# A planner that counts TensorE's instructions as they arrive, and a third MLP block begun in another bank

## The chip, the cores and the metric

The kernel runs on one core of one Trainium2 chip. The metric is device time in microseconds (us) of one execution. Engines are called as in the profile: PE is TensorE (PEld its weight loads), ACT is ScalarE, DVE is VectorE, POOL is GpSimd, SP is SyncE, whose queue issues nearly all DMAs here.

## The reference

```python
def _attn_ref(q, k, v):                       # (8 batch entries, 8 heads, 576, 64)
    scores = 1.0 / np.sqrt(D) * np.matmul(q, k.transpose(0, 1, 3, 2))
    rel = pos[:, None] - pos[None, :]
    mask_plain = (rel >= 0) & (rel < 32)                       # heads 0 to 3
    mask_dil = (rel >= 0) & (rel < 128) & (rel % 4 == 0)       # heads 4 to 7
    scores = np.where(masks[None], scores, -1e9)
    attn = softmax(scores)                    # maximum taken off, sum + 1e-9 below
    return np.matmul(attn, v)
def _moe_ref(x, w_in, w_out):                 # x (4608, 512), w_in (512, 2048), w_out (2048, 512)
    h = x @ w_in
    g = h * (1.0 / (1.0 + np.exp(-1.702 * h)))
    return g @ w_out
```

The MLP reads the attention's output, tokens by 512 (8 heads of 64). q, k and v are f32, the weights f64.

## The kernel before

**The MLP** is the bulk of the work. Each f32 operand is split into a high and a low part that PE can multiply at full rate (`xh`, `xl` of the tokens, `wih`, `wil`, `woh`, `wol` of the weights, `gh`, `gl` of the gated values), and each product is made of three matmuls (high·high, low·high, high·low). Tokens go in groups of 512: `m0` to `m7` are the first 512 tokens of the eight batch entries, `r` is the 64 left of each, 8 x 64. The inner dimension of 2048 goes in 16 blocks `f`. `Group.up(f)` makes 12 matmuls (four chunks `c` of 128 inputs, three each) into the PSUM tile `hp`; ACT takes the tanh of it (L613), DVE the gate (L616), ACT or DVE the high part `gh` (L234 or L236), DVE or POOL the low part `gl` (L241). `Group.down(f)` adds 12 matmuls into four accumulators `acc`. There is one `hp` bank, so `up(f + 1)` waits for the gate of `f`; in the first group alone, `f == 1` uses the bank `sp`, which is otherwise the attention's scores.

**The weights** arrive as f64 words cut into u64, and each of the 32 tiles (`decode(n)`, even `n` w_in, odd `n` w_out) is decoded on the way in: three ACT passes (L289, L290, L283; the last can be a DVE one, L285), then on DVE a shift (L293) and an add (L295), a cast to the high part (ACT or DVE) and a subtraction for the low part (L241, DVE or POOL). Five buffers hold raw tiles: `cell0` to `cell2`, and the two halves of `second`; two more raw tiles pass through `bt` and the buffer `qk`. All decoding falls into the first group's time.

**The attention** of one batch entry is four pairs of heads (`k`, four for each entry). `scores` (L369 for the mask, L383, 88 or 76 small matmuls) write `sp`; DVE takes maximum (L402), subtracts (L241), ACT the exponential (L406), DVE the sum (L420), its reciprocal (L410, L412), POOL or DVE multiplies `pr` by it, DVE transposes into `ct`. For the first entry, `first_product` (L470) multiplies `ct` by `v` straight into `first_x`, four PSUM banks that hold the outputs of two pairs in turn; ACT copies the high part `xh` out of it, DVE subtracts for `xl`. The first entry's four pairs must be through before the first group's four chunks are there. Later entries go through `bt` and the bank `av` (L484), and run beside the group before them.

**The order.** `Plan` holds every step with a cost for each engine that may run it, an urgency, what it reads and writes. `ordered` plays the engines forward with these costs and lists the steps in the order in which they would start; each engine's program is then fixed in that order, and an engine that waits for one step's input holds back all steps behind it. SP's DMAs are steps of the same list. `LATER` adds to the planned end of a step on an engine when an engine is chosen for it, and `AHEAD` lets an urgent step be waited for. Where PE is planned to have nothing for over half a microsecond, and the planned time is below `WARM`, `ordered` puts in idle products (`warm`, L727: `ident` times `ident` into the unused bank `av`, 512 columns), which keep PE's clock up.

## Time and profile before

| | |
|---|---|
| runs before, median of 3 (lowest to highest) | 900.85 us (900.6 to 901.49) |
| the profiled execution's own time | 900.52 us |
| its span, first to last instruction | 898.4 us |
| mean granted clock of PE | 0.992 |
| PE busy, share of the span | 98% |
| DVE, ACT, POOL busy | 51%, 43%, 6% |

A row of the timeline gives start, duration and the number of like instructions that follow one another; in brackets stands how long the engine had been idle and who ended that. "issue" means that it waited for nothing that the profile shows. Matmul durations overlap (a row of 0.39 us starts 0.23 us after the one before it), so PE's pace is read from the starts. In the table of stretches PEclk is the granted clock of PE, 1.00 being full speed.

### The profile page before, as it was taken

Reading aid. Unit: us, or ns where it says so; the run is one execution under the profiler, and the core shown is the slowest. Engines: PE = TensorE matmul, PEld = TensorE weight load, DVE = VectorE, ACT = ScalarE, POOL = GpSimd, SP = SyncE. Lnnn points to the kernel's source line nnn. Section 1 sums busy time; section 2 is a strip of 40 time slices with the busy share of each in tenths; the row PEclk is TensorE's granted clock in tenths of the full one; section 3 lists DMA queues with packets and bytes.
Section 4 is the critical chain, followed back from the end, with each engine's and each line's share of the span. In section 5 each row is a group of like instructions: output and inputs, shape, how many; then the busy total and the mean of one; then the engine's idle time right before and its main releaser. Section 6 shows DMA issues by size and latency. Waiting matters only on the chain.

```text
span 898.4 us, 17202 instructions
## 1 busy us (share of the span) xinstructions
PE 883.9 (98%) x7352; PEld 718.3 (80%) x7352; DVE 461.6 (51%) x858; ACT 390.1 (43%) x680; POOL 50.2 (6%) x61
## 2 busy tenths in 40 slices
PE   7899999999999999999999999999999999999998
PEld 4577878888888888888888888888888888888886
DVE  5899986666566336652566255634622322232222
ACT  6888984343443234432543245333532322232222
POOL 2131001000001001000000000000100000000000
PEclk9899999999999999999999999999999999999999
DMA  9358743131223003110331022200100010002001
GB/s 356 101 179 254 196 171 125 48 93 47 71 71 94 1 9 133 48 47 0 96 92 47 1 94 60 81 1 20 49 1 1 1 47 1 1 1 47 1 1 47
DMA packets 35804, 61.34 MB, mean 68 GB/s; under 512 B 17424, under 2 KB 17680, under 8 KB 35728
## 3 DMA queue, kind: packets, MB, share of 16 engines
q1 hardware_dynamic: 35584, 60.11, 21.0%
q8 instruction: 58, 0.95, 0.5%
q14 instruction: 18, 0.15, 0.1%
q10 hardware_dynamic: 144, 0.13, 0.0%
HBM read 49.48 MB, written 9.44 MB: 66 GB/s over the span
## 4 chain that ended last, share of the span: by engine, by line
PE 92%; ACT 3%; DMA 2%; DVE 2%; issue 1%; SPq 0%; DVEq 0%; ACTq 0%
PE hp_m L605 38%; PE acc_m L641 13%; PE acc_m L642 13%; PE acc_m L645 12%; PE hp_r L605 5%; PE av L484 3%; PE sp L383 3%; PE acc_r L642 2%; PE acc_r L641 2%; PE acc_r L645 2%; DMA cell<-wi_dram 1%; DMA second<-wi_dram 1%; ACT words L289 0%; PE first_x L470 0%; PE sp L484 0%
## 5 line engine op out<-in xcount | busy, mean ns | idle before, releaser
L605 PE MATMUL hp_m<-xh,wih 128*128 128x512 f32 x512 | 201.5, 394 | 2.9 <-ACT woh L234 2.2
L641 PE MATMUL acc_m<-gh,woh 128*128 128x512 f32 x512 | 201.6, 394 | 0.3 <-ACT gh L234 0.3
L616 DVE SCALAR_TENSOR_TENSOR g_m<-g_m,hp_m 128x512 f32<-128x512 f32 x128 | 87.7, 685 | 220.7 <-ACT g_m L613 220.5
L605 PE MATMUL hp_m<-xh,wil 128*128 128x512 f32 x512 | 200.1, 391 | 0.0
L605 PE MATMUL hp_m<-xl,wih 128*128 128x512 f32 x512 | 199.9, 391 | 0.0
L642 PE MATMUL acc_m<-gh,wol 128*128 128x512 f32 x512 | 199.8, 390 | 0.0
L613 ACT ACTIVATE g_m<-hp_m 128x512 f32<-128x512 f32 x128 | 76.5, 597 | 247.0 <-PE hp_m L605 242.8
L645 PE MATMUL acc_m<-gl,woh 128*128 128x512 f32 x512 | 143.4, 391 | 0.0
L605 PEld LDWEIGHTS hp_m<-xh,wih 128*128 128x128 f32 x512 | 96.2, 188 | 24.6 <-ACT woh L234 2.6
L241 DVE TENSOR_TENSOR gl<-g_m,gh 128x512 fp32r<-128x512 f32 x126 | 89.8, 713 | 50.7 <-ACT gh L234 49.4
L641 PEld LDWEIGHTS acc_m<-gh,woh 128*128 128x128 f32 x512 | 96.5, 189 | 21.4 <-ACT gh L234 0.7
L605 PEld LDWEIGHTS hp_m<-xl,wih 128*128 128x128 f32 x512 | 96.4, 188 | 20.4 <-DVE xl L241 0.3
L605 PEld LDWEIGHTS hp_m<-xh,wil 128*128 128x128 f32 x512 | 96.4, 188 | 20.2 <-DVE wil L241 0.7
L642 PEld LDWEIGHTS acc_m<-gh,wol 128*128 128x128 f32 x512 | 96.6, 189 | 19.7
L645 PEld LDWEIGHTS acc_m<-gl,woh 128*128 128x128 f32 x512 | 95.5, 188 | 20.1
L234 ACT ACTIVATE gh<-g_m 128x512 fp32r<-128x512 f32 x113 | 71.2, 630 | 67.5 <-DVE g_m L616 67.4
L241 POOL TENSOR_TENSOR pr<-pr,sm 128x320 f32<-128x320 f32 x45 | 40.1, 901 | 546.6 <-DVE sm L412 541.8
L234 ACT ACTIVATE bt<-ct 32x320 f32<-32x320 f32 x102 | 47.9, 470 | 11.1 <-DVE ct L433 9.3
L406 ACT ACTIVATE pr<-pr 128x640 f32<-128x640 f32 x32 | 23.7, 740 | 41.1 <-DVE pr L241 40.5
L616 DVE SCALAR_TENSOR_TENSOR g_r<-g_r,hp_r 128x512 f32<-128x512 f32 x16 | 11.0, 687 | 50.7 <-ACT g_r L613 50.7
L234 ACT ACTIVATE xm<-av 128x512 f32<-128x512 f32 (+2 forms) x42 | 23.7, 596 | 28.8 <-PE av L484 16.6
L420 DVE TENSOR_REDUCE sm<-pr 128x10 f32<-128x640 f32 x32 | 26.1, 816 | 16.7 <-ACT pr L406 16.7
(119 smaller groups left out, 839.0 us busy)
## 6 DMA issues: line engine op xcount, KB each, us to landing
qk<-qk_dram SPq DMA_DIRECT2D x17, 576.0 KB, 4.5
out_dram<-ost_m SPq DMA_DIRECT2D x31, 256.0 KB, 2.1
second<-qk_dram SPq DMA_DIRECT2D x13, 576.0 KB, 5.0
v<-vp_dram SPq DMA_DIRECT2D x32, 216.0 KB, 4.6
words<-vp_dram SPq DMA_DIRECT2D x24, 216.0 KB, 4.3
cell<-wi_dram SPq DMA_DIRECT2D x10, 512.0 KB, 6.6
cell<-wo_dram SPq DMA_DIRECT2D x9, 512.0 KB, 5.6
second<-wo_dram SPq DMA_DIRECT2D x6, 512.0 KB, 4.9
```

What stands on the lines that cost most here:

```text
L234: A.activation(dst, src, AF.Copy, scale=scale)
L241: (V if e == DVE else G).tensor_tensor(out=dst, in0=a, in1=b, op=op)
L383: T.matmul(dst[:, w:w + n], u["qk"][rows, at:at + 32], u["qk"][rows, S + first:S + first + n], start=not masked(k), stop=True, tile_positi ...
L406: add({ACT: 0.75}, urgency, lambda e: A.activation(prs[y], prs[y], AF.Exp, scale=0.125), (), (PR,))
L420: add({DVE: 0.80}, urgency, lambda e: V.tensor_reduce(out=sm, in_=pr, axis=AX.X, op=ALU.add), (PR,), (SM,))
L484: T.matmul(dst, u["v"][a][0:KW, m], bt[0:KW, a, m], start=True, stop=True, skip_group_check=True)
L605: T.matmul(hps[f], st[:, f, c], mv[:, c], start=c == 0 and k == 0, stop=c == NC - 1 and k == 2)
L613: A.activation(self.g32, hps[f], AF.Tanh, scale=0.851)
L616: V.scalar_tensor_tensor(out=self.g32, in0=self.g32, scalar=1.0, in1=hps[f], op0=ALU.add, op1=ALU.mult)
L641: T.matmul(self.acc[j], woh[:, f, cols], gh, start=f == 0, stop=False)
L642: T.matmul(self.acc[j], wol[:, f, cols], gh, start=False, stop=False)
L645: T.matmul(self.acc[j], woh[:, f, P * j:P * j + P], self.g[f][1], start=False, stop=f == NF - 1)
```

## The change

Four things are edited. (1) The planner gets a model of PE's instructions arriving in blocks: steps of PE carry a `count` of instructions, and `fetched` lets a step that crosses an edge (193, then every 256) begin its rest no sooner than the next block is there. (2) Idle products that are planned before 12 us are of 128 columns and four times as many. (3) In the first group, block `f == 2` goes into the bank `av`, and the second entry's attention and the last eight decodes, which stood behind block 1, stand behind block 2; idle products end where this block starts. (4) The planner's numbers change: `AHEAD`, `WARM`, DVE's entry of `LATER`, and the urgencies of the first loads, of the decodes (`32.0 + 1.92 * n` for `28.0 + 2.62 * n`) and of the second entry's attention (`52.0 + 9.4 * c` for `43.0 + 8.2 * c`).

```diff
-AHEAD = 0.70
-WARM = 36.0
+AHEAD = 0.36
+WARM = 60.0
+SHORT = 12.0
...
-LATER = {PE: 0.0, ACT: 0.0, DVE: 0.40, POOL: 0.0, DMA: 0.0}
+LATER = {PE: 0.0, ACT: 0.0, DVE: 0.49, POOL: 0.0, DMA: 0.0}
...
+        issued, blocks = [0], [0.0]
...
+        def fetched(count, when, cost):
+            n = issued[0]
+            issued[0] += count
+            for j in range(len(blocks) - 1, 1 << 30):
+                edge = 193 + 256 * j
+                if edge >= n + count or edge > 1500:
+                    return when + cost
+                part = cost * (edge - n) / count
+                at = max(when + part, blocks[j])
+                blocks.append(at + (6.1 if at < 18.0 else 4.2))
+                when, cost, n, count = at, cost - part, edge, count - (edge - n)
...
-                idle = max(0, int((when - max(free[e], 1.2) - 0.5) / (0.26 if when > 8.0 else 0.44)))
-                order.extend([(None, e)] * idle)
+                short = when < SHORT
+                size = (0.26 if when > 8.0 else 0.44) * (0.25 if short else 1.0)
+                idle = max(0, int((when - max(free[e], 1.2) - 0.5) / size))
+                fetched(2 * idle, max(free[e], 1.2), idle * size)
+                order.extend([(None if short else -1, e)] * idle)
             order.append((i, e))
+            if e == PE:
+                cost = fetched(ops[i][5], when, cost) - when
...
-        add({DMA: 524}, {0: -8.1, 1: -6.2, 2: -5.2, 3: -4.5}.get(n, urgency), fetch, (), (R, R + "l", *taken))
+        add({DMA: 524}, {0: -8.6, 1: -7.4, 2: -5.1, 3: -2.2}.get(n, urgency), fetch, (), (R, R + "l", *taken))
...
-        add({DMA: 590}, (-9.0, -8.0, -6.0, -4.0)[k] if k < NC else 1.6 * k - 2.0, work, waits(k), (place, place + "l"))
+        add({DMA: 590}, (-9.0, -6.6, -3.2, -2.1)[k] if k < NC else 1.6 * k - 2.0, work, waits(k), (place, place + "l"))
...
-        add({DMA: 390 if k < NC else 442}, (-5.5, -3.0, -2.0, -1.0)[k] if k < NC else 1.6 * k - 0.3, work, waits(k),
-            (place, place + "l"), (0.0, 1.0, 5.0, 14.0)[k] if k < NC else 0.0)
+        add({DMA: 390 if k < NC else 442}, (-7.8, -6.4, -4.9, -1.4)[k] if k < NC else 1.6 * k - 0.3, work, waits(k),
+            (place, place + "l"), (0.0, 0.0, 4.0, 6.0)[k] if k < NC else 0.0)
...
-            place = "sp" if self is main[0] and f == 1 else "hp"
+            place = {1: "sp", 2: "av"}.get(f, "hp") if self is main[0] else "hp"
...
-                decode(n, 28.0 + 2.62 * n)
+                decode(n, 32.0 + 1.92 * n)
...
-            if nxt == 1 and f == 1:
+            if nxt == 1 and f == 2:
                 for c in range(NC):
-                    attention(NC + c, 43.0 + 8.2 * c)
+                    attention(NC + c, 52.0 + 9.4 * c)
...
-    def warm(e):
-        if "av" not in pairs[NC]:
+    def warm(i):
+        if 2 not in main[0].hps:
             if "idle" not in misc:
                 misc["idle"] = bank([P, GT], "av", "idle")
-            T.matmul(misc["idle"], ident, ident[:, None, :].broadcast_to([P, GT // P, P]), start=True, stop=True)
+            n = 1 if i is None else GT // P
+            T.matmul(misc["idle"][:, 0:P * n], ident, ident[:, None, :].broadcast_to([P, n, P]), start=True, stop=True)
```

Smaller edits: the first entry's steps get counts of 180 and 184 and new costs (1.5, and 2.3 for the first, in place of 1.6 and 2.1), the MLP's steps counts of 6, 4 and 2; the first two decodes' urgencies are 1.0 higher. Lines of the changed kernel are 22 to 24 further down than those of the profile.

The edits work through the order. PE's program has 98 more instructions of idle products ahead of the third pair's scores: 20, 43 and 8 products (two instructions each) before the scores of pairs 0, 1 and 2, where there were 5, 7 and 10; the idle products that stood before the first pair's product (6) are gone.

SP's first loads before (`qk_0`, `second`, `xm`, `xr` are the queries and keys of pairs 0 to 3; `v_0` and the second load of `second` are the values of pairs 0 and 1; `cell0`, `cell2` and `cell1`, `bt` are raw w_in and w_out tiles 0 and 1):

```order
L326 DMA qk_0_124<-qk_dram 128x1152
L279 DMA cell0_112<-wi_dram 128x512
L326 DMA second_111<-qk_dram 128x1152
L279 DMA cell1_113<-wo_dram 128x512
L326 DMA xm_76<-qk_dram 128x1152
L339 DMA v_0_130<-first_v_dram 128x768
L279 DMA cell2_114<-wi_dram 128x512
L279 DMA bt_86<-wo_dram 128x512
L326 DMA xr_77<-qk_dram 128x1152
```

and now:

```order
L348 DMA qk_0_124<-qk_dram 128x1152
L301 DMA cell0_112<-wi_dram 128x512
L361 DMA v_0_127<-first_v_dram 128x768
L301 DMA cell1_113<-wo_dram 128x512
L348 DMA second_111<-qk_dram 128x1152
L361 DMA second_111<-first_v_dram 128x768
L301 DMA cell2_114<-wi_dram 128x512
L348 DMA xm_76<-qk_dram 128x1152
L301 DMA bt_86<-wo_dram 128x512
L348 DMA xr_77<-qk_dram 128x1152
```

The queries and keys of pair 1 moved from third to fifth place, behind the values of pair 0 and the raw w_out tile 0; those of pair 2 from fifth to eighth; w_in tile 1 (`cell2`) stays seventh.

DVE before, from the reciprocal of pair 1's sums (`sm1`) to that of pair 2's (`sm0`); `xr` and `xl` read pair 0's product, the transposes make pair 1's `ct`:

```order
L412 RECIPROCAL sm1_83<-sm1_83 128x10
L241 TENSOR_TENSOR pr1_79<-pr1_79,sm1_83 128x320
L236 COPY xr_77<-first_x_90 128x64
L429 STREAM_TRANSPOSE ct1_85<-pr1_79 128x320
L241 TENSOR_TENSOR xl_71<-first_x_90,xh_70 128x432
L241 TENSOR_TENSOR xl_71<-first_x_90,xh_70 128x80
L429 STREAM_TRANSPOSE ct1_85<-pr1_79 128x320
L420 TENSOR_REDUCE sm0_82<-pr0_78 128x10
L402 TENSOR_REDUCE mx1_81<-sp_3_397 128x10
L410 TENSOR_SCALAR sm0_82<-sm0_82 128x10
L241 TENSOR_TENSOR pr1_79<-sp_3_397,mx1_81 128x640
L412 RECIPROCAL sm0_82<-sm0_82 128x10
```

and now, over the same stretch:

```order
L434 RECIPROCAL sm1_83<-sm1_83 128x10
L317 ISA words_115<-cell2_114,words_115 128x1024
L315 TENSOR_SCALAR words_115<-words_115 128x512
L442 TENSOR_REDUCE sm0_82<-pr0_78 128x10
L263 TENSOR_TENSOR xl_71<-first_x_90,xh_70 128x432
L263 TENSOR_TENSOR xl_71<-first_x_90,xh_70 128x80
L451 STREAM_TRANSPOSE ct1_85<-pr1_79 128x320 x2
L424 TENSOR_REDUCE mx1_81<-sp_3_442 128x10
L432 TENSOR_SCALAR sm0_82<-sm0_82 128x10
L263 TENSOR_TENSOR pr1_79<-sp_3_442,mx1_81 128x640
L434 RECIPROCAL sm0_82<-sm0_82 128x10
```

The sum of pair 2 (`sm0<-pr0`) stood behind four steps that read pair 0's product or its high part; now it stands ahead of them, and POOL does both of pair 1's multiplications, and ACT the copy to `xr`.

PE before, from the first block's last chunk (`hp_m0_0`; `hp_m0_1` and `hp_m0_2` are the second and third block):

```order
L605 MATMUL hp_m0_0_454<-xh_70,wih_66 128x512
L605 MATMUL hp_m0_0_454<-xh_70,wil_67 128x512
L605 MATMUL hp_m0_0_454<-xl_71,wih_66 128x512
L605 MATMUL hp_m0_1_655<-xh_70,wih_66 128x512
L605 MATMUL hp_m0_1_655<-xh_70,wil_67 128x512
L605 MATMUL hp_m0_1_655<-xl_71,wih_66 128x512
L605 MATMUL hp_m0_2_698<-xh_70,wih_66 128x512
L605 MATMUL hp_m0_2_698<-xh_70,wil_67 128x512
L605 MATMUL hp_m0_2_698<-xl_71,wih_66 128x512
L641 MATMUL acc_m0_0_708<-gh0_72,woh_68 128x512
L642 MATMUL acc_m0_0_708<-gh0_72,wol_69 128x512
```

and now:

```order
L628 MATMUL hp_m0_0_506<-xh_70,wih_66 128x512
L628 MATMUL hp_m0_0_506<-xh_70,wil_67 128x512
L628 MATMUL hp_m0_0_506<-xl_71,wih_66 128x512
L628 MATMUL hp_m0_1_569<-xh_70,wih_66 128x512
L628 MATMUL hp_m0_1_569<-xh_70,wil_67 128x512
L628 MATMUL hp_m0_1_569<-xl_71,wih_66 128x512
L628 MATMUL hp_m0_2_714<-xh_70,wih_66 128x512
L628 MATMUL hp_m0_2_714<-xh_70,wil_67 128x512
L628 MATMUL hp_m0_2_714<-xl_71,wih_66 128x512
L628 MATMUL hp_m0_3_756<-xh_70,wih_66 128x512
L628 MATMUL hp_m0_3_756<-xh_70,wil_67 128x512
L628 MATMUL hp_m0_3_756<-xl_71,wih_66 128x512
```

Before, one chunk of the third block stood behind the last chunks of the first two, in the bank of the first, and the accumulation of block 0 followed; now three chunks of the third block are already done at this place, its fourth follows, and two chunks of a fourth block come before the accumulation.

More of the change, by code (lines that the diff above doesn't have):

```diff
@@ L47, in __init__, with add @@
         self.ops, self.writer, self.readers = [], {}, {}
-    def add(self, costs, urgency, work, reads=(), writes=(), slack=0.0):
+    def add(self, costs, urgency, work, reads=(), writes=(), slack=0.0, count=0):
         i, after = len(self.ops), set()
@@ L133, in ordered @@
                         open_[to].add(j)
-        return [(warm if i is None else ops[i][2], e) for i, e in order]
+        return [(ops[i][2] if i is not None and i >= 0 else lambda e, i=i: warm(i), e) for i, e in order]
 @with_exitstack
```

17 lines of the change are left out of this document (9 added, 8 removed).

## The prediction

> **What bounds the kernel now.** I read the page's shares first, then PE's waits, then a table of stretches (its columns: stretch, length, busy time of PE, PEld, DVE, ACT, POOL, granted clock, DMA share, GB/s), then the timelines where PE lost time.
>
> ```profile
> span 898.4 us, 17202 instructions
> ...
> PE 883.9 (98%) x7352; PEld 718.3 (80%) x7352; DVE 461.6 (51%) x858; ACT 390.1 (43%) x680; POOL 50.2 (6%) x61
> ```
>
> ```profile
> PE hp_m L605 <- ACT woh L234: 2.2, 1, 2.2
> PE first_x L470 <- issue: 1.9, 1, 1.9
> ...
> PE sp L383 <- issue: 1.1, 1, 1.1
> ```
>
> ```profile
> 10.00:20.00 10.00, 7.24 (x247) 4.37 (x247) 8.20 (x17) 7.37 (x10) 3.97 (x4) 0.99 1.02 407
> 20.00:30.00 10.00, 8.73 (x231) 5.61 (x231) 6.01 (x15) 6.29 (x12) 1.40 (x2) 0.50 0.35 124
> ...
> 40.00:50.00 10.00, 7.84 (x27) 5.59 (x25) 9.01 (x18) 8.20 (x13) 0.00 (x0) 0.83 0.60 175
> ...
> 117.00:135.00 18.00, 16.98 (x72) 12.96 (x71) 17.38 (x33) 15.98 (x29) 0.00 (x0) 1.00 0.37 121
> 135.00:800.00 665.00, 665.00 (x5302) 549.15 (x5301) 320.43 (x596) 251.01 (x465) 27.97 (x31) 1.00 0.15 46
> ```
>
> PE bounds it: from 135 to 800 us it is never idle, at full clock. The change takes no work out of that stretch, so the time moves only by what PE loses before 135. Three losses can be read there: the first entry's attention, in which PE waits twice for nothing that the profile shows ("issue") and runs at half clock from 20 to 30; a wait of 2.2 before the third MLP block, with the clock at 0.83 about it; and 1.0 of idle time from 117 to 135, while DVE is busy 17.38 of 18 us and ACT 15.98. The 98% hides the first of these, because idle products count as busy.
>
> ```profile
> 6.66 3.15 PE L727 MATMUL idle<-ident 128*128 128x512 bf16 x7
> 9.62 0.46 PE L369 MATMUL sp<-plain,ident 128*128 128x320 bf16 x2
> ...
> 14.06 1.10 PE L383 MATMUL sp<-xm 64*32 64x32 f32 x88
> ...
> 17.46 0.77 PE L470 MATMUL first_x<-ct,v 32*64 32x32 f32 x50 [0.67 <-DVE ct L429]
> 20.18 0.92 PE L470 MATMUL first_x<-ct,v 32*64 32x64 f32 x40 [1.95 <-issue]
> ...
> 24.18 0.24 PE L383 MATMUL sp<-xr 64*32 64x16 f32 x2 [1.09 <-issue]
> ...
> 25.92 1.67 PE L470 MATMUL first_x<-ct,second 32*64 32x32 f32 x92
> ...
> 31.77 1.08 PE L470 MATMUL first_x<-ct,xm 32*64 32x64 f32 x80
> ...
> 35.89 1.08 PE L470 MATMUL first_x<-ct,xr 32*64 32x64 f32 x80 [0.77 <-DVE xl L241]
> ...
> 41.06 0.40 PE L605 MATMUL hp_m<-xl,wih 128*128 128x512 f32 x1
> 43.62 0.62 PE L605 MATMUL hp_m<-xh,wih 128*128 128x512 f32 x1 [2.16 <-ACT woh L234]
> ...
> 47.25 0.40 PE L642 MATMUL acc_m<-gh,wol 128*128 128x512 f32 x1
> ...
> 112.69 1.15 PE L484 MATMUL av<-bt,v 96*64 96x64 f32 x32
> ...
> 122.01 0.39 PE L605 MATMUL hp_m<-xh,wih 128*128 128x512 f32 x1
> ...
> 123.83 0.39 PE L605 MATMUL hp_m<-xl,wih 128*128 128x512 f32 x1
> ```
>
> The last two rows are eight matmuls apart: 0.2275 us each at full speed. The two "issue" rows cut steps in the middle. With two instructions a product, 700 stand ahead of the first cut in PE's order (28 idle products, 270 of three scores, 52 of pair 0's product) and 956 ahead of the second: 256 apart. So I take it that code comes in blocks, with edges at 444 and 1212 too. Instruction 444 ran near 14.2, 20 products into pair 2's scores; the block behind 700 came at 20.18, 6.0 later, while loads ran at 407 GB/s, and the next 4.0 after that.
>
> ```profile
> 40.80 0.60 ACT L613 ACTIVATE g_m<-hp_m 128x512 f32<-128x512 f32 x1
> ```
>
> ```profile
> 42.80 0.68 DVE L616 SCALAR_TENSOR_TENSOR g_m<-g_m,hp_m 128x512 f32<-128x512 f32 x1
> ```
>
> The wait of 2.2 is put down to `woh`, but these two rows show the bank: block 0's gate ended at 43.48, and the third block, which wants block 0's bank, began at 43.62. The tanh had ended at 41.40; DVE's queue held the gate until 42.80.
>
> **The change part by part.** These rows of ACT, DVE and POOL carry the terms:
>
> ```profile
> 13.70 0.69 ACT L289 ACTIVATE words<-cell 128x512 f32<-128x512 f32 x1 [1.22 <-DMA cell<-wi_dram]
> ...
> 33.77 1.37 ACT L283 ACTIVATE second<-second 128x512 f16<-128x512 f32 x1
> 34.87 0.69 ACT L234 ACTIVATE wih<-words 128x512 fp32r<-128x512 f32 x1
> ...
> 37.01 1.11 ACT L234 ACTIVATE xh<-first_x 128x512 fp32r<-128x512 f32 x1 [0.19 <-PE first_x L470]
> ```
>
> ```profile
> 23.32 0.78 DVE L420 TENSOR_REDUCE sm<-pr 128x10 f32<-128x640 f32 x1
> ...
> 26.05 0.20 DVE L412 RECIPROCAL sm<-sm 128x10 f32<-128x10 f32 x1
> ...
> 39.13 1.07 DVE L241 TENSOR_TENSOR xl<-first_x,xh 128x512 fp32r<-128x512 f32 x1
> ...
> 51.64 0.83 DVE L402 TENSOR_REDUCE mx<-sp 128x10 f32<-128x640 f32 x1 [0.54 <-PE sp L383]
> ...
> 128.45 0.69 DVE L295 CUSTOM_DVE_ANT_0 words<-cell,words 128x1024 uint16<-128x1024 uint16 x1
> 129.05 0.43 DVE L293 TENSOR_SCALAR words<-words 128x512 uint32<-128x512 uint32 x1
> ...
> 131.86 0.69 DVE L295 CUSTOM_DVE_ANT_0 words<-second,words 128x1024 uint16<-128x1024 uint16 x1
> ...
> 134.25 0.68 DVE L241 TENSOR_TENSOR wol<-words,woh 128x512 fp32r<-128x512 f32 x1
> ```
>
> ```profile
> 50.99 1.30 POOL L241 TENSOR_TENSOR wol<-words,woh 128x512 fp32r<-128x512 f32 x1 [12.06 <-ACT woh L234]
> ```
>
> *1. The first attention.* Pair 1's queries and keys move from third to fifth. The seventh load had landed at 13.70, in both orders 3.74 MB in; the fifth is 1.12 MB earlier, 2.75 us at 407 GB/s: 10.95. Its scores start near 11.2, where they started at 9.62. The 43 short idle products ahead of them should cost a quarter each of the 0.45 that the cold row shows (3.15 for 7): 4.8 from 6.7 on, to 11.5. So the load covers them but for 0.3; if the load were early, they would be the price. They also bring edge 444 into these scores, at 12.4 in place of 14.2: the block behind 700 should come at 18.4. Pair 2's scores need the eighth load, 1.4 behind the seventh: 15.2 to 16.7, where they ended at 15.16 before. Pair 0's product then starts, is cut after 9 products, goes on at 18.4 and needs 1.1 to 1.5 for the other 83 (1.67 for 92 cold, 1.08 for 80 warm): 19.5 to 19.9, was 21.10. Pair 3's scores meet edge 956 half way and go on 4.0 to 6.0 after 18.4, to end at 23.0 to 25.0, was 24.42. DVE's order no longer holds pair 2's sum (23.32) behind pair 0's `xl`, but its reciprocal still follows pair 3's subtraction: 24.9 to 26.9, was 26.05. Pair 1's product meets edge 1212 after 80 of 92, 4.0 after the edge before: it ends at 26.6 to 28.6, was 27.59. `xl` (0.64), a transpose (0.43) and pair 2's product (1.08) end at 29.4 to 31.3, was 32.85. Then come `xh`, `xl` and the fourth product, 1.1 each, and whatever ACT's queue has ahead of `xh` (two sign passes of 1.1): 33.4 to 34.7 for the fourth product's end, was 36.97. I take 34.0, a little nearer the early end since 4.0 is what the block without loads beside it took: **-3.0**. Ends: -0.5, if each block comes 6.0 after the one before (18.4, 24.4, 30.4, and 6 us of work behind); -4.6, if edges cost nothing.
>
> *2. Two products more ahead of that end*, in place of idle ones: 2 x 3 x 0.2275 = **-1.4**. Their weights are the first decodes, long done.
>
> *3. The third block's bank.* 43.62 - 41.06 - 0.23 = 2.33 goes: **-2.3**. What is late next: from 34.0 PE has five chunk products (3.4), reaches the last chunks at 37.4, and needs the fourth chunk's `xl`, which ended 3.2 behind the fourth product before (36.97 to 40.20) and so comes at 37.2. Three products (2.05) later, at 39.5, the fourth block wants block 0's bank. Block 0's last product ends at 38.1; tanh, gate and two hand-overs of 0.2 make 39.8; with the 1.4 that DVE's queue held the gate, 41.2. I take a wait of 0.6, nearer the first, because in DVE's order only an add and a shift stand just ahead of the gate: **+0.6**, ends 0 and 2.2.
>
> *4. The clock.* From 43.62 to 47.25 eight matmuls took 3.63 instead of 1.82, at the half clock that followed the wait: **-1.8**. If the shorter waits bring it on too, 0.
>
> PE's lead is then 7.9.
>
> *5. Given back until 135.* Decoding must keep up. DVE reached pair 4's maximum at 51.64, with 9 of its 32 adds (L295) behind it. In the changed order PE gets there by four chunk products, 12 accumulations and scores (1.4 + 2.7 + 1.4 + 1.3) behind the wait that ends at 40.1: 46.9, and 10 adds stand ahead. A decode holds DVE for about 1.5 (0.60 from the add's start to the shift's, at most 0.43 and 0.68 for shift and subtraction). So DVE leads by 4.7 + 1.5 = 6.2, which is 1.7 short of PE's lead. From there to the last decode DVE has 9 instructions fewer than before, about 3 us (two halves of `pr` and two `gl` went to POOL), but ACT 7 more, about 1 us on an engine that was busy 15.98 of 18. I take 1.7 + 1.0 = **+2.7**; ends 0 and 7.9. SP's eight copies into `bt` for each pair stand among the loads as before.
>
> *6. Costed at nothing:* the planner's numbers after 135. POOL gets one of four `xl` splits at each change of group, and both halves of `pr`. It is busy 27.97 of 665 us, and PE has 12 products (2.7) of the old group meanwhile. If that cover is gone, seven changes lose at most the 0.6 each by which POOL's 1.30 is above DVE's spacing: 4.2.
>
> Sum: -3.0 - 1.4 - 2.3 + 0.6 - 1.8 + 2.7 = -5.2. The profiled execution took 900.52 (span 898.4 and 2.1 around it), which gives 895.3; the runs' median is 0.33 higher: **895.6**.
>
> [...]
>
> **The rivals.**
>
> *Decoding gives everything back.* For it: DVE and ACT are nearly full from 117 to 135, and an early PE then only waits for weights. Against it: DVE itself is 6.2 ahead. It decides if DVE's last decode still ends near 134.9; then **900.8**.
>
> *Nothing is given back:* 900.85 - 7.9 = **892.9**. For it: only 1.0 of waits from 117 to 135, and 3 us less for DVE.
>
> *Edges cost nothing in the new order,* since fewer loads lie ahead of the blocks: **894.0**. Against it: the block behind 956 came as loads thinned, and still took 4.0.
>
> *The count does nothing:* blocks come as late as before, part 1 is 0, and a PE that leads by 4.9 gives back 1.7: **897.6**.
>
> *Slower: the second entry's fourth pair.* Its urgency goes from 67.6 to 80.2, and its product stands behind 336 MLP matmuls where 270 stood (112.69): at PE's pace 121 to 124. If its copies into `bt` come later than that, PE waits with the whole end of the first group behind it. It decides from 7.0 us of lateness on (the 5.2 gained and 1.8); at 8 us **903.6**.
>
> **How the numbers follow.** A measurement of this kernel can tell 0.2% (1.8 us) from no change. The forecast, 893.4 to 898.0, has 0.56; nothing given back 0.12; edges for nothing 0.05; a count that does nothing 0.05; everything given back 0.15; slower 0.07. Faster is the first four, 0.78; same 0.15; slower 0.07. The range leaves out the slower case, under half of the case about zero and a third of the two fastest, 0.2 in all: 892.3 to 901.0.
>
> **What would show it.** The "issue" row in pair 0's product ends near 18.4 (20.18), the fourth product near 34 (36.97). No wait before `hp_m` near 40 reaches 2 us, and the clock from 40 to 50 is 1.00. DVE's last L295 ends at 126 to 129 (132.55). The forecast is wrong if blocks come 6 us apart all the way, if DVE holds block 0's gate as long as before, or if PE's waits from 50 to 135 add up to over 5 us.

## The result and the profile after

The changed kernel takes 893.98 us (median of 4 runs, 892.98 to 895.7) against 900.73 before: ratio 0.9927, 95% interval 0.9911 to 0.9942. Run once more beside other kernels it took 894.62, ratio 0.9934 (0.9921 to 0.9947). The forecast was 895.6. Three executions on record took two to over three times as long as the others (one of e1 3038.32, one of e2 1879.94, one of the kernel before 3078.14) and are left out of every comparison. The profiled execution took 894.24, 6.28 less than the one before; its page and its PE waits:

```profile
span 892.5 us, 17271 instructions
...
PE 878.6 (98%) x7386; PEld 719.4 (81%) x7386; DVE 446.0 (50%) x823; ACT 394.6 (44%) x684; POOL 77.8 (9%) x92
```

```profile
PE sp L405 <- issue: 3.3, 1, 3.3
PE first_x L492 <- issue: 1.6, 1, 1.6
PE sp L405 <- DMA second<-qk_dram: 1.5, 1, 1.5
...
PE hp_m L628 <- DVE g_m L639: 0.2, 1, 0.2
```

The wait of 2.2 before the third block is gone (a wait of 0.2 for the gate is left), but the two waits for nothing that the profile shows (the cuts, since each stops PE in the middle of a step) add up to 4.9, where they made 3.0. The table of stretches (columns as in the prediction):

```profile
20.00:30.00 10.00, 6.69 (x187) 4.88 (x188) 7.83 (x17) 7.31 (x17) 4.57 (x6) 0.50 0.47 159
...
40.00:50.00 10.00, 9.78 (x94) 7.45 (x96) 10.00 (x19) 10.00 (x17) 0.00 (x0) 1.00 0.88 312
...
117.00:135.00 18.00, 18.00 (x111) 14.76 (x110) 16.04 (x28) 12.57 (x22) 7.83 (x6) 1.00 0.39 112
```

From 40 to 50 the clock is 1.00 (0.83 before), from 117 to 135 PE is never idle (16.98 of 18 before), with DVE and ACT less busy and POOL at 7.83 instead of nothing. From 20 to 30 nothing has improved: the clock is still 0.50, and PE is busy 6.69 (8.73 before). The timeline of PE at the places of the prediction:

```profile
17.93 1.39 PE L492 MATMUL first_x<-ct,v 32*64 32x32 f32 x82 [1.64 <-issue]
...
24.12 0.95 PE L405 MATMUL sp<-xr 64*32 64x64 f32 x44 [3.31 <-issue]
...
29.77 1.93 PE L751 MATMUL idle<-ident 128*128 128x512 bf16 x4
...
32.41 1.08 PE L492 MATMUL first_x<-ct,xm 32*64 32x64 f32 x80
...
36.51 1.08 PE L492 MATMUL first_x<-ct,xr 32*64 32x64 f32 x80 [0.59 <-DVE xl L263]
...
43.51 0.50 PE L628 MATMUL hp_m<-xh,wih 128*128 128x512 f32 x1 [0.22 <-DVE g_m L639]
```

The first cut ends at 17.93, 2.25 earlier than before; yet the fourth product ends at 37.59, 0.62 later (36.97).

To place the 5.9 us of span (898.4 to 892.5) I count PE's matmuls of the MLP (idle and attention matmuls left out). The 44th is ahead of the second entry's attention in both kernels; ahead of the 373rd stands all of it, again in both. These four rows are the 44th and the 373rd before, and the same two now:

```profile
49.77 0.39 PE L605 MATMUL hp_m<-xh,wil 128*128 128x512 f32 x1
...
139.25 0.39 PE L605 MATMUL hp_m<-xh,wih 128*128 128x512 f32 x1
```

```profile
45.24 0.39 PE L665 MATMUL acc_m<-gh,wol 128*128 128x512 f32 x1
...
132.50 0.39 PE L628 MATMUL hp_m<-xh,wih 128*128 128x512 f32 x1
```

So 4.53 came up to the 44th, another 2.22 from there to the 373rd (89.48 down to 87.26), and 0.85 was lost behind it (759.15 to 760.0). Up to 135 us nothing of the lead was given back.

### The profile page after: what moved, and what is told of

Its sections match the earlier page's. It is cut to its first block, busy times and chain, and to the rows that moved or that the text cites. A ratio compares the mean times of both kernels' runs of the same rounds, so it can differ in the third digit from the quotient of the medians.

```text
span 892.5 us, 17271 instructions
## 1 busy us (share of the span) xinstructions
PE 878.6 (98%) x7386; PEld 719.4 (81%) x7386; DVE 446.0 (50%) x823; ACT 394.6 (44%) x684; POOL 77.8 (9%) x92
## 4 chain that ended last, share of the span: by engine, by line
PE 96%; DVE 1%; DMA 1%; issue 1%; ACT 0%; SPq 0%; DVEq 0%
PE hp_m L628 39%; PE acc_m L664 13%; PE acc_m L668 13%; PE acc_m L665 13%; PE hp_r L628 5%; PE av L506 3%; PE sp L405 3%; PE acc_r L665 2%; PE acc_r L664 2%; PE acc_r L668 2%; DMA second<-qk_dram 1%; PE first_x L492 0%; PE sp L506 0%; DVE words L317 0%; PE sp L391 0%
## 5 line engine op out<-in xcount | busy, mean ns | idle before, releaser
L256 ACT ACTIVATE gh<-g_m 128x512 fp32r<-128x512 f32 x125 | 79.1, 633 | 73.8 <-DVE g_m L639 73.6
L263 POOL TENSOR_TENSOR pr<-pr,sm 128x320 f32<-128x320 f32 x64 | 50.6, 811 | 350.4 <-DVE sm L434 347.8
```

The source lines that it names most:

```text
L256: A.activation(dst, src, AF.Copy, scale=scale)
L263: (V if e == DVE else G).tensor_tensor(out=dst, in0=a, in1=b, op=op)
```

## The experiments

The runs' own times are compared by the ratio to the kernel before, each with its 95% interval. In the summary below, the 44th and the 373rd matmul are those of each one's profiled execution, whose own time stands beside them; where that is above the median, the early part of it was late.

| kernel | median us | ratio (interval) | profiled | 44th | 373rd |
|---|---|---|---|---|---|
| before | 900.73 | 1 | 900.52 | 49.77 | 139.25 |
| changed | 893.98 | 0.9927 (0.9911 to 0.9942) | 894.24 | 45.24 | 132.50 |
| e1, changed, bank undone | 897.51 | 0.9965 (0.9951 to 0.9978) | - | - | - |
| e2, before + bank | 900.45 | 0.9997 (0.9988 to 1.0006) | 900.45 | 49.98 | 138.77 |
| e3, changed, no arrival, no short products | 894.18 | 0.9934 (0.9922 to 0.9947) | 896.85 | 47.97 | 135.28 |
| e4, changed, old due times | 895.92 | 0.9940 (0.9927 to 0.9954) | 896.67 | 47.45 | 135.10 |
| e5, before + bank + AHEAD + LATER | 899.71 | 0.9988 (0.9976 to 0.9999) | 899.28 | 48.85 | 137.56 |
| e6, before + bank + AHEAD | 899.00 | 0.9982 (0.9973 to 0.9991) | 899.32 | 46.75 | 138.39 |
| e7, changed, LATER undone from 45 us | 894.86 | 0.9939 (0.9926 to 0.9953) | 894.81 | 45.60 | 133.62 |
| e8, changed, again | 894.62 | 0.9934 (0.9921 to 0.9947) | 894.80 | 45.69 | 133.27 |
| e9, changed, reciprocal off the port | 898.44 | 0.9976 (0.9967 to 0.9985) | 897.88 | 47.05 | 136.10 |
| e10, changed, gap of 6.1 up to 26 us | 897.02 | 0.9957 (0.9944 to 0.9970) | 896.90 | 46.90 | 134.97 |
| e11, changed, old loads | 898.26 | 0.9973 (0.9962 to 0.9985) | 898.05 | 47.35 | 136.49 |
| e12, e5 + due times | 898.17 | 0.9967 (0.9957 to 0.9977) | 897.76 | 48.29 | 135.93 |

**The bank.** First undone in the changed kernel, then done alone in the kernel before.

```diff
-            place = {1: "sp", 2: "av"}.get(f, "hp") if self is main[0] else "hp"
+            place = {1: "sp"}.get(f, "hp") if self is main[0] else "hp"
...
-        if 2 not in main[0].hps:
+        if "av" not in pairs[NC]:
```

> The changed kernel with the third block's accumulator back in the bank that the first block used (and the idle products allowed until the second entry's first product). Theory (the bank is what the wait and the clock drop at 40 to 50 us hung on, 2.3 + 1.8 less 0.6): the products of the third block stand behind the gate of the first again, at about 43.5 us, the granted clock of 40:50 falls under 0.95, and the time is about 897.4 (3.5 above the changed kernel's 894.0). Rival (what is gained ahead of 50 us is taken back by the weights' adds until 135 us anyway): 894.0 to 895.0, with waits for wi or wo shrinking between 50 and 135 by as much as the lead shrank.

897.51: the bank is worth about 3.1 us with all the rest there (0.9965 against 0.9927 and 0.9934). Of this kernel's profile only the order of instructions is used: on ACT, DVE and POOL it is the changed kernel's up to where that stands at 52, 55 and 61 us, so up to there no new order of these engines comes with the old bank; behind it the orders differ. On PE, idle products stand where the third block was begun; what they cost can't be told apart from the bank. The clock and the waits from 40 to 50 that the theory names are not shown.

```diff
-            place = "sp" if self is main[0] and f == 1 else "hp"
+            place = {1: "sp", 2: "av"}.get(f, "hp") if self is main[0] else "hp"
...
-        if "av" not in pairs[NC]:
+        if 2 not in main[0].hps:
...
-            if nxt == 1 and f == 1:
+            if nxt == 1 and f == 2:
```

> The kernel before with the bank of the third block alone changed (bank of the second entry's accumulator, the second entry's attention written behind the third block, idle products until the third block begins). Theory of the bank, each term kept: 900.7 - 3.5 = about 897.2, with no wait for the first gate and a clock of 0.95 or more in 40:50. Theory of the later numbers (the order of decoding and of the second entry's attention is what keeps the lead): the lead at 48 us is 3 or more, but the adds stand at about 131.9 us as before, most of the lead is given back until 135 us, and the time is 899.5 to 900.7.

900.45, no change. My second theory had the right time for a wrong reason: no lead at 48 us was given back, there never was one. PE and DVE in this kernel:

```profile
42.31 0.50 PE L605 MATMUL hp_m<-xh,wih 128*128 128x512 f32 x1 [0.67 <-ACT wih L234]
44.34 0.79 PE L605 MATMUL hp_m<-xh,wil 128*128 128x512 f32 x1 [1.53 <-DVE wil L241]
```

```profile
43.59 0.69 DVE L241 TENSOR_TENSOR wil<-words,wih 128x512 fp32r<-128x512 f32 x1
```

The third block no longer waits for its bank (free at 43.48 before), but for its weights, whose low part ends at 44.28. In the kernel before the same subtraction stood right behind the bank's release and ended at 44.08, just ahead of the block's second product (44.13), so it could have been read there:

```profile
43.39 0.69 DVE L241 TENSOR_TENSOR wil<-words,wih 128x512 fp32r<-128x512 f32 x1
```

In the changed kernel the same subtraction runs 6.9 earlier, so there the bank counts:

```profile
36.71 0.67 DVE L263 TENSOR_TENSOR wil<-words,wih 128x512 fp32r<-128x512 f32 x1
```

**Arrival and short products.** All counts 0, `SHORT = 0.0`, idle products no longer counted:

```diff
-SHORT = 12.0
+SHORT = 0.0
...
-        self.ops.append((costs, (urgency, i), work, after - {None, i}, slack, count))
+        self.ops.append((costs, (urgency, i), work, after - {None, i}, slack, 0))
...
-                fetched(2 * idle, max(free[e], 1.2), idle * size)
```

> The changed kernel without the arrival of instructions in the plan (counts 0) and without short idle products. Theory (arrival and short products moved the cuts but not the end of the first attention: 37.59 us against 36.97 before): the fourth first product ends at 36.5 to 38.0, a cut of 1.5 us or more stands in the first product or the fourth pair's scores, and the time is 894.0 within 1.0. Rival (the arrival in the plan gave what was gained after 48 us too, by placing work where PE waits): 895.5 to 897.

894.18: in time, what gives the change its first name gave nothing that can be told. The clocks of the single executions say that this may be a balance of two things. The four of e3 that were not profiled took 893.83 to 894.79 at a mean granted clock of 0.996 to 0.998; the profiled one took 896.85 at 0.994, and the changed kernel's ten had 0.990 to 0.994. Worked out from these means, an estimate, PE was at half clock for 4 to 7 us in the four and for 11 to 18 in the changed kernel. So the count or the short products may have gained in the order what they lost in the clock. That stays open, and the two were not undone apart.

**The due times** of the decodes and of the second entry's attention:

```diff
-                decode(n, 32.0 + 1.92 * n)
+                decode(n, 28.0 + 2.62 * n)
...
-                    attention(NC + c, 52.0 + 9.4 * c)
+                    attention(NC + c, 43.0 + 8.2 * c)
```

> The changed kernel with two lines of numbers as before: decoding due at 28.0 + 2.62 n and the second entry's attention at 43.0 + 8.2 c (instead of 32.0 + 1.92 n and 52.0 + 9.4 c). The order up to 50 us is the same. Theory (these numbers gave the 2.1 us gained between 48 and 135 us where a loss was forecast, and more): the lead at 48 us is as in the changed kernel, waits for wi or wo or the banks stand between 60 and 135, and the time is 896 to 898.5. Rival (the third block's bank and the earlier start feed the later stage by themselves, or LATER's 0.49 and the work that went to POOL did it): 893.5 to 894.8.

Unclear as a time: 895.92, but the interval overlaps the changed kernel's. The trace, of its slowest execution, says where the time went. From the 44th to the 373rd it takes 87.65 (87.26 and 87.58 in the changed kernel's two profiles), with no wait for weights: there the theory fell. The 2 us by which it trails the changed kernel's profiles (47.45 for 45.24 and 45.69) are lost before the 44th, where the order is the same as in the changed kernel; more on that under e8.

**The two planner rules with the bank**, in the kernel before:

```diff
-AHEAD = 0.70
+AHEAD = 0.36
...
-LATER = {PE: 0.0, ACT: 0.0, DVE: 0.40, POOL: 0.0, DMA: 0.0}
+LATER = {PE: 0.0, ACT: 0.0, DVE: 0.49, POOL: 0.0, DMA: 0.0}
```

> The kernel before with three edits: the third block's bank, AHEAD 0.36 and LATER 0.49; no arrival of instructions, no short idle products, all due times and the order of loads as before. Theory (the two rules decide in which order VectorE, ScalarE and GpSimd decode, and so have the third block's weights ready when its bank is; the rest of the change gave nothing): 894.0 within 1.2, at least 9 inner products ahead of the fourth first product's end, no wait over 0.5 us at 40 to 48 and none at 130. Rival (the arrival, the due times and the order of loads carry the gain): 897 to 900.5, with the third block waiting for its weights at 42 to 45 as in the kernel with the bank alone.

899.71: the rival, in its mechanism too: the third block waits 1.02 for its weights, at 41.30. With AHEAD alone beside the bank:

```diff
-AHEAD = 0.70
+AHEAD = 0.36
```

> The kernel before with the third block's bank and AHEAD 0.36 only (LATER 0.40). Theory (AHEAD brings the third block's decoding ahead, LATER keeps the adds on time at 130 us): the third block starts before 43 us without a long wait, the lead at 48 us is 2.5 or more over the kernel before, a wait of 0.8 us or more for wi or wo stands at 115 to 135, time 897 to 899. Rival (LATER plays no part): 894 to 896.5. Rival (AHEAD plays no part): 900 to 901.

899.00, as forecast in time, and for the reason given only in part: a lead of 3.0 at the 44th is there (46.75), and 91.64 from there to the 373rd give most of it back, but in waits for `gh` (0.56 at 48.60, 0.20 at 101.14), for `bt` (0.29 at 71.44) and for gates (0.62 at 73.22, 0.79 at 95.21), none of them at 115 to 135.

**LATER late.** In the changed kernel, 0.40 for all that DVE would start after 45 us:

```diff
-                    if e == min(ops[i][0], key=lambda k: start(i, k) + abs(ops[i][0][k]) + LATER[k]):
+                    if e == min(ops[i][0], key=lambda k: start(i, k) + abs(ops[i][0][k]) + (0.40 if k == DVE and start(i, k) > 45.0 else LATER[k])):
```

> The changed kernel with LATER back at 0.40 for all that VectorE would start after 45 us; everything up to there in the same order. Theory (at 0.49 VectorE hands more of the decoding to GpSimd, 7.8 us of it in 117:135 where there was none, and so the adds keep ahead): a wait for wi or wo of 0.8 us or more at 100 to 135, and the loss between 48 and 135 us grows from 3.15 to 4.5 or more, time 895.3 to 896.5. Rival (the earlier third block and decoding alone gave it): 893.5 to 894.6.

894.86, the same. POOL is busy 21.24 from 48 to 135 (22.25 with 0.49), so the edit moved hardly any work, PE waits for nothing there, and the theory that LATER hands the decoding to POOL fell.

**The loads.** Undone in the changed kernel:

```diff
-        add({DMA: 524}, {0: -8.6, 1: -7.4, 2: -5.1, 3: -2.2}.get(n, urgency), fetch, (), (R, R + "l", *taken))
+        add({DMA: 524}, {0: -8.1, 1: -6.2, 2: -5.2, 3: -4.5}.get(n, urgency), fetch, (), (R, R + "l", *taken))
...
-        add({DMA: 590}, (-9.0, -6.6, -3.2, -2.1)[k] if k < NC else 1.6 * k - 2.0, work, waits(k), (place, place + "l"))
+        add({DMA: 590}, (-9.0, -8.0, -6.0, -4.0)[k] if k < NC else 1.6 * k - 2.0, work, waits(k), (place, place + "l"))
...
-        add({DMA: 390 if k < NC else 442}, (-7.8, -6.4, -4.9, -1.4)[k] if k < NC else 1.6 * k - 0.3, work, waits(k),
-            (place, place + "l"), (0.0, 0.0, 4.0, 6.0)[k] if k < NC else 0.0)
+        add({DMA: 390 if k < NC else 442}, (-5.5, -3.0, -2.0, -1.0)[k] if k < NC else 1.6 * k - 0.3, work, waits(k),
+            (place, place + "l"), (0.0, 1.0, 5.0, 14.0)[k] if k < NC else 0.0)
```

> The changed kernel with the due times of the first loads (q and k, v, the first four packed weight blocks) as before. Theory (the order of loads carries what the rules and the bank alone lacked): third block late by a wait for its weights at 38 to 45 us or a lead at 48 us smaller by 1.5 or more, time 896 to 899. Rival (the due times of decoding and of the second entry's attention carry it): 893.8 to 895.2.

898.26, in the theory's range: the loads are worth about 3.8 (0.9973 against 0.9927 and 0.9934), more than the bank. Of the theory's two signs the smaller lead is there (47.35 at the 44th, 2.11 behind the changed kernel), the wait for weights is not. PE's waits there:

```profile
42.50 0.50 PE L628 MATMUL hp_m<-xl,wih 128*128 128x512 f32 x1 [0.78 <-DVE xl L263]
...
45.30 0.50 PE L628 MATMUL hp_m<-xh,wih 128*128 128x512 f32 x1 [0.92 <-DVE g_m L639]
```

Another 1.2 goes in a wait for a gate at 124.05. The other side is e5 with the due times on top:

```diff
-            decode(c - 1, c + 0.1)
+            decode(c - 1, c + 1.1)
...
-                decode(n, 28.0 + 2.62 * n)
+                decode(n, 32.0 + 1.92 * n)
...
-                    attention(NC + c, 43.0 + 8.2 * c)
+                    attention(NC + c, 52.0 + 9.4 * c)
```

> The kernel before with the bank, AHEAD 0.36 and LATER 0.49, and the due times of decoding and of the second entry's attention; order of loads as before, no arrival, no short products. Theory (the loads carry it): 898.5 to 900, as without the due times (899.7). Rival (the due times carry it): 894 to 896, with the loss between 48 and 135 us at 3.5 or less (4.6 without them).

PE's waits in this one:

```profile
40.73 0.47 PE L605 MATMUL hp_m<-xh,wih 128*128 128x512 f32 x1 [1.00 <-DVE wih L236]
...
46.58 0.50 PE L641 MATMUL acc_m<-gh,woh 128*128 128x512 f32 x1 [0.85 <-ACT gh L234]
```

898.17, between the two expectations and nearer the theory's 898.5 to 900: 1.9 better than without the due times (e5). What separates it from e3 (894.18) is the loads, two step costs and `WARM`. With the old loads either the fourth chunk's `xl` and the gate come late (e11) or the third block's weights (e12). As new due times for loads make the planner write another order for every engine, whether the transfers themselves or that order is what counts stays open.

**The same program twice.** The changed kernel, nothing altered:

> The changed kernel once more, nothing altered. Theory (PE's cuts at the start come when instructions happen to arrive, which differs from run to run): the cuts with no releaser between 10 and 30 us stand at other instructions or have other lengths than 1.64 and 3.31 us, the loss at 48 us differs from 25.8 by up to 2.5, and the loss between 48 and 135 us is 3.15 within 0.4; median 894.0 within 0.8. Rival (the cuts are fixed by the count of instructions): 1.6 and 3.3 us within 0.3 at the same two instructions.

894.62. These are the cuts and the second, third and fourth product of this profile, and then of e4, whose order on PE, DVE, ACT, POOL and SP is the same up to 50 us:

```profile
20.29 1.49 PE L492 MATMUL first_x<-ct,v 32*64 32x32 f32 x82 [4.35 <-issue]
...
25.66 0.94 PE L405 MATMUL sp<-xr 64*32 64x64 f32 x44 [2.39 <-issue]
...
28.11 1.67 PE L492 MATMUL first_x<-ct,second 32*64 32x32 f32 x92
...
32.85 1.08 PE L492 MATMUL first_x<-ct,xm 32*64 32x64 f32 x80
...
36.98 1.08 PE L492 MATMUL first_x<-ct,xr 32*64 32x64 f32 x80 [0.63 <-DVE xl L263]
```

```profile
20.82 1.49 PE L492 MATMUL first_x<-ct,v 32*64 32x32 f32 x82 [4.36 <-issue]
...
25.92 0.94 PE L405 MATMUL sp<-xr 64*32 64x64 f32 x44 [2.12 <-issue]
...
28.37 1.82 PE L492 MATMUL first_x<-ct,second 32*64 32x32 f32 x92
...
34.58 1.08 PE L492 MATMUL first_x<-ct,xm 32*64 32x64 f32 x80
...
38.71 1.08 PE L492 MATMUL first_x<-ct,xr 32*64 32x64 f32 x80 [0.63 <-DVE xl L263]
```

The cuts stand at the same instructions each time (82 products of the first pair, 44 of the fourth pair's scores), and their lengths change: 1.64 and 3.31, 4.35 and 2.39, 4.36 and 2.12. Both later profiles have one more cut 128 products ahead of the first, in the second pair's scores (0.61 and 1.17, ending at 11.64 and 12.18); the first profile has none there, where these scores waited for their load until 11.33. So the edges are fixed by the count, and the arrival is not. How far does a late arrival reach? The second profile is 2.36 later than the first at the first cut, 1.54 at the second and 1.39 at the end of the second product (29.78 for 28.39), but only 0.47 at the end of the fourth. e4 is 0.53 and 0.26 later than the second profile at the cuts, 0.41 at the end of the second product (30.19), and 1.73 at the end of the fourth. Both times most of the change falls between the end of the second product and the start of the third. The granted clock shows why. These are the stretches around its fall and return, before, in the changed kernel's first profile, in its second and in e4:

```profile
19.00:20.00 1.00, 0.00 (x0) 0.00 (x0) 0.12 (x1) 0.10 (x1) 0.70 (x1) 0.94 1.01 400
...
30.00:31.00 1.00, 1.00 (x5) 0.71 (x4) 1.00 (x4) 1.00 (x1) 0.00 (x0) 0.94 0.56 225
```

```profile
18.00:19.00 1.00, 1.00 (x78) 1.00 (x82) 0.97 (x3) 0.97 (x2) 0.45 (x1) 0.54 1.00 400
...
31.00:32.00 1.00, 1.00 (x4) 0.81 (x3) 0.84 (x3) 1.00 (x2) 1.00 (x2) 0.63 0.39 152
```

```profile
16.00:18.00 2.00, 0.00 (x0) 0.00 (x0) 1.83 (x3) 1.97 (x5) 1.28 (x1) 0.90 1.06 412
...
31.00:32.00 1.00, 1.00 (x6) 0.49 (x5) 1.00 (x5) 1.00 (x2) 0.56 (x1) 0.88 0.64 217
```

```profile
20.00:21.00 1.00, 0.18 (x11) 0.18 (x18) 1.00 (x2) 0.02 (x1) 1.00 (x2) 0.86 1.02 410
...
34.00:35.00 1.00, 1.00 (x40) 0.48 (x41) 0.23 (x1) 0.10 (x1) 0.21 (x1) 0.82 0.06 16
```

Away from its fall and return the clock reads 0.50 or 1.00 (before, 0.50 from 20 to 30 and 1.00 from 135 to 800), so a stretch of 1.00 with a mean of 0.63 was at half clock for 0.74 of it, and so on: half clock ran from 19.88 to 30.12 before, from 18.08 to 31.74, from 17.60 to 31.24, and from 20.72 to 34.36. That is 10.24 before and 13.66, 13.64 and 13.64 now: one step of 3.4 more. Between the second and the third product PE does the same ten matmuls without a wait (six of the MLP, four idle), in 4.02, 3.07 and 4.39 us in the three profiles of the changed order (third product at 32.41, 32.85 and 34.58). With the time at half clock counted half, that is 2.3 of full clock in each. So the arrival passes through to the second product, and the time at which full clock comes back does the rest: 34.36 in e4, 3.1 later than in the second profile (31.24).

**Two tries at the first attention.** On DVE the third pair's reciprocal stands behind the fourth pair's maximum, which waits for the cut scores. One edit makes the plan put it ahead. In the plan, POOL's steps and those DVE steps whose cost is written below zero take turns (the list `port`), an assumption of the plan that no run here tests; a cost above zero takes a step out of that:

```diff
-        add({DVE: -0.15}, urgency, lambda e: V.tensor_scalar(
+        add({DVE: -0.15 if k != 2 else 0.15}, urgency, lambda e: V.tensor_scalar(
```

> The changed kernel with one cost in the plan of another sign: the first step of the third pair's reciprocal no longer waits for the port shared with GpSimd in the plan, so that on VectorE it stands ahead of the fourth pair's max (which waits for the cut scores) instead of behind it. Theory (the end of the first attention hangs on the order on VectorE and on the clock, not on the arrival itself): the third pair's reciprocal runs before 24 us (26.7 in the changed kernel), its weights are ready before 29, the third first product starts 2 us or more earlier than 32.4 and the fourth ends at 34 to 36; time 891.5 to 893.2. Rival (the cut at 24 to 26 us and the half clock behind it set the end whatever the order): the fourth ends within 0.8 us of 37.8, time 893.8 to 895.

898.44: slower than the changed kernel. PE in its profile:

```profile
30.65 1.08 PE L492 MATMUL first_x<-ct,xm 32*64 32x64 f32 x80
...
35.96 1.08 PE L492 MATMUL first_x<-ct,xr 32*64 32x64 f32 x80 [0.89 <-DVE xl L263]
...
45.09 0.50 PE L664 MATMUL acc_m<-gh,woh 128*128 128x512 f32 x1 [2.38 <-ACT gh L256]
```

```profile
23.87 0.22 DVE L434 RECIPROCAL sm<-sm 128x10 f32<-128x10 f32 x1
...
34.83 1.08 DVE L263 TENSOR_TENSOR xl<-first_x,xh 128x512 fp32r<-128x512 f32 x1
```

The reciprocal comes 2.84 earlier (26.71) and the third product 1.76. The fourth follows by 0.55 only: it waits for the third's `xl`, which stands behind a cast and an add of decoding on DVE (1.47 and 0.67 from 32.84 on). And the plan, played anew from there, left no products of the fourth block ahead of the first block's accumulation, which waits 2.38 for `gh`; half clock follows (six matmuls from 46.62 to 49.19 start 0.43 apart, and the clock has a mean of 0.83 from 40 to 50). Correcting the plan's arrival fared no better:

```diff
-                blocks.append(at + (6.1 if at < 18.0 else 4.2))
+                blocks.append(at + (6.1 if at < 26.0 else 4.2))
```

> The changed kernel with the plan's gap between two blocks of instructions 6.1 us up to 26 us (4.2 from 18 us on in the changed kernel; the trace has 6.2 and 5.1 to 5.4). The plan then puts the second first product ahead of the first block's first step, the third pair's reciprocal ahead of the fourth pair's max, and 15 products of the MLP ahead of the fourth first product's end. Theory as in the kernel with the reciprocal off the port: the fourth first product ends at 34 to 36.5, time 891 to 893. Rival: the end stays within 0.8 us of 37.8 but more products lie ahead of it, time 893 to 895.

897.02: the second pair's product moved ahead and was now cut itself, for 1.51 at 29.48. No kernel tried is faster than the changed one.

## Why the prediction was right, and where it was not

The time was 1.6 below the forecast, inside its range, but two of its steps failed and made up for one another. That the number came out is luck; steps 2 to 4 came out as worked out.

- **Step 1, the first attention: failed**, -3.0 forecast, +0.6 measured (37.59 for 36.97), outside its ends. The first cut ended at 17.93, near the forecast 18.4. The next came 6.2 behind it (24.12), the late end of my two, where I had leaned to 4.0; the fourth pair's scores ended just past their range for it (25.07), the second product late in its range (28.39). Here the loss against the kernel before is already 0.8 (27.59): the block came as it did there (24.18), but 44 products of the scores stood behind the edge, not 2 (0.95 for 0.24; my sum had them at 0.6). Then my chain broke: the third product was to start at 28.3 to 30.2, and started at 32.41. (Even that range has 0.6 more than the `xl` of 0.64 and the transpose of 0.43 that I named for it.) I had left out the multiplication by the reciprocal, which with its transposes and the `xl` between them lets `ct` be done by 31.19 only:

```profile
26.71 0.21 DVE L434 RECIPROCAL sm<-sm 128x10 f32<-128x10 f32 x1
...
30.30 0.89 DVE L451 STREAM_TRANSPOSE ct<-pr 128x320 f32<-128x320 f32 x2
```

```profile
27.06 1.85 POOL L263 TENSOR_TENSOR pr<-pr,sm 128x320 f32<-128x320 f32 x2 [4.39 <-DVE sm L434]
```

And PE's own order, which I had left out too, ended last: without a wait it does three matmuls of the MLP, four idle products and three more of the MLP up to 32.41, most of it at half clock, which lasted one step longer than before.

More than the sizes, the principle failed: I passed the cut's gain on to the end one for one and took no account of the clock, and the repeat shows that 2.36 at the first cut move the end by 0.47. Two smaller misreadings did no harm. In the new order 3.54 MB, not 3.74, lie up to the seventh load, and the third pair's scores came earlier (14.93 to 16.03) than my 15.2 to 16.7. The short idle products cost 0.063 each (28 in 1.76), not 0.11, but PE then waited 1.51 for the load. From the third product's start to the fourth's it took 4.10, close to my 3.4 to 4.0; in e9, with a third product 1.76 earlier, 5.31.

- **Step 2, two products more ahead of the end:** 12 matmuls instead of 6, as forecast, -1.4.
- **Step 3, the bank, right in size:** the wait of 2.33 is gone, and the new one cost 0.38 over PE's pace, with 0.6 forecast. That it hangs on the third block's weights I had not said; e2 shows that without them it gives no gain.
- **Step 4, the clock, right:** 1.00 from 40 to 50, -1.8.
- **Step 5, given back until 135: wrong sign**, +2.7 forecast, -2.2 measured. Its formula was PE's lead less DVE's 6.2. With the lead that was there, 4.5 and not 7.9, it gives nothing back; the first error caused this part of the second. The 1.0 for ACT's seven instructions more never showed (busy 12.57 of 18 us, 15.98 before). And I left out that the kernel before had waits of its own there to lose:

```profile
125.86 1.07 PE L645 MATMUL acc_m<-gl,woh 128*128 128x512 f32 x4
127.19 0.50 PE L641 MATMUL acc_m<-gh,woh 128*128 128x512 f32 x1 [0.25 <-ACT gh L234]
...
132.09 0.84 PE L645 MATMUL acc_m<-gl,woh 128*128 128x512 f32 x3
133.66 0.50 PE L605 MATMUL hp_m<-xh,wih 128*128 128x512 f32 x1 [0.73 <-DVE g_m L616]
```

Read from the starts, as PE's pace is, they cost more than the 1.0 in brackets: the four products from 125.86 on took 1.33, for 0.91 at 0.2275 each, and the three from 132.09 on took 1.57, for 0.68. With 0.1 for the product behind each wait, and 0.4 that the two products from 120.94 to 121.78 took too long, this is 1.9 of the 2.2. In the changed kernel PE waits for nothing there. Of the longer wait the rows show the cause:

```profile
132.28 0.60 ACT L613 ACTIVATE g_m<-hp_m 128x512 f32<-128x512 f32 x1 [1.21 <-PE hp_m L605]
```

```profile
132.91 0.69 DVE L616 SCALAR_TENSOR_TENSOR g_m<-g_m,hp_m 128x512 f32<-128x512 f32 x1 [0.36 <-ACT g_m L613]
```

ACT and DVE both stood idle for this gate, so neither's queue held it: PE's order had only three accumulations between the two blocks; the changed kernel has twelve between the two that it does there (129.78 to 132.50). DVE's last add of decoding starts at 127.81, 4.05 earlier (131.86), and ends inside my 126 to 129. Which edit gave the better order here stays open: the stretch takes 87.65 without the due times (e4) and 87.63 with the old loads (e12), but 89.14 in e11.

- **Step 6, nothing behind 135:** +0.85 measured, 0.6 of it up to PE's last matmul and 0.2 behind that, small against its end of 4.2.

So the rival "nothing is given back" was nearest in what follows the lead. The lead itself was that of "the count does nothing" (4.9, measured 4.5), whose 897.6 charges 1.7 given back where the formula of step 5 gives at most the 1.0 for ACT. "Edges cost nothing" has the measured time, 894.0, by luck: the edges cost 4.9, and the gain came elsewhere. As to the causes, the prediction spoke of the instruction count, the bank and the clock; the runs put next to nothing on the count (e3), 3.1 on the bank if the rest is there (e1) and nothing if it isn't (e2), and 3.8 on the due times of the loads with the order that the planner made of them (e11), which I had read only for the second pair's scores. These amounts hold with the rest in place and don't add up to the whole.

## What to carry to other kernels

A wait that ends with one releaser may have a second one just behind it: before a bank is given, look up when the other inputs of the waiting step are ready (here 44.08 against 43.48). A gain at an early step is passed on only as far as the next queue and the clock let it (here 1.39 at the second product became 0.44 at the third); follow it through each engine's order, and take "given back" as lead less slack, worked out again when the lead changes. Where a planner writes the order, an edit of one number is an edit of all that follows: judge it by the time where it acts and the time as a whole, and expect local repairs to be lost further on (e9, e10).

## What the runs showed of the hardware

- PE's half clock lasted 10.24 before (19.88 to 30.12) and in e9 (19.22 to 29.46), and 13.66, 13.64 and 13.64 in the three profiles of the changed order: three and four times 3.41 us. The one behind the wait of 2.16 in the kernel before lasted 3.42 (43.78 to 47.20). In the three profiles of the changed order half clock began at 18.08, 17.60 and 20.72 and ended at 31.74, 31.24 and 34.36. The 3.1 between the last two ends moved the third product by 1.3 of its 1.7, in programs that are the same up to there, with the cuts' ends within 0.53.
- PE was cut at edges 256 instructions (128 products) apart, at the same instructions in programs that are the same up to there, and the cuts ended at times that differ by up to 2.9 us (17.93 to 20.82 at one edge). A cut lasted up to 4.36. That the instructions behind an edge arrive as a block is the author's reading: the rows name no releaser. In the kernel's time the length of a cut is hardly seen here (894.24 with a first cut of 1.64, 894.80 with 4.35).
- Idle products and the clock, before: the 3.10 us between the third and the fourth product (32.79 to 35.89), 2.33 of them filled by ten idle products, passed at 1.00 (31 to 42); behind the wait of 2.16, with none in it, came the half clock from 43.78.
- The MLP's products of high and low parts start 0.2275 us apart at a clock of 1.00 (before, 122.01 to 123.83), the bf16 idle products of the same 512 columns 0.22 apart (before, from 32.79: ten in 2.33, the last of them 0.38).
